# Mirror rows scattered four at a time, and three more split units a batch, in a Fourier-mixing and maxout kernel

## The chip, the cores and the metric

The kernel runs on one core of one Trainium2 chip. The metric is the device time of one execution in microseconds; lower is better. Before the change the median of three runs is 394.58 us (394.48 to 395.24).

## What is computed

```python
def _attn_ref(x):                      # x: 8 x 3072 x 256, float32
    X = np.fft.fft(x, axis=1)
    X = np.fft.fft(X, axis=2)
    return X.real.astype(np.float32)

def _moe_ref(x, w1, w2, w3, w_out):    # x: 24576 x 256; w1..w3: 256 x 768; w_out: 768 x 256
    h = np.maximum(np.maximum(x @ w1, x @ w2), x @ w3)
    return (h @ w_out).astype(np.float32)
```

The output of the first is the input of the second, its eight batches of 3072 rows laid one behind another. The result is 24576 rows of 256 float32.

## The kernel before

**Mirror.** The input is real, so row k and row 3072 - k of a batch's transform are made of the same even part and the same odd part, once added and once subtracted. The kernel computes the parts for k from 0 to 1536 and gets two rows of the output from each, a plus row and a minus (mirror) row. `tE` and `tO` hold the parts for 1536 values of k as columns, `te_tab` and `to_tab` the cosines and sines for them. The one k that is left over is done by `Mix.end` and `l2_mid`.

**Order of the columns.** The 1536 columns are ordered by residue: 96 columns with k = r mod 32 for r = 1, then for r = 2, and so on (`ramp`, `kvec`), with the residues 0, 16 and half of 15 at the end. A matmul of `Mix.k` (L466) has one residue's columns as moving data, and `_parts` lists them for each 512 columns. `_runs` says which rows of the output a slot of 128 columns holds.

**Units.** A batch has three blocks of 512 columns and six chunks of 128 hidden units; one block and chunk make a unit, so a batch has 18 units, numbered u = 0 to 17 here, and the kernel 144 (`g`). A unit that is not split multiplies both parts with two combined weight matrices into two PSUM banks (`unit_plus`, L490 and L491), takes the maximum through `stmp` on ScalarE (L503) and VectorE (L504) into `hp`, then adds one more product to each bank (`unit_minus`, L497), which turns the plus columns into minus columns, and takes the maximum into `hm`: six matmuls of 512 columns. A split unit does the third weight matrix apart: `third` (L819, L821) computes its even and odd products once, VectorE makes `even` (L824), ScalarE `odd` (L823), and GpSimd adds and subtracts them (L828, `plus` and `minus`). What is left is one bank, with its maximum in one VectorE instruction (L837 for `hp`, L849 for `hm`): five matmuls. `third` of a unit is issued two units ahead. Odd units from 7 on are split. A split unit's bank comes from `ps_l1`; the others take one from `ps_l1` and one from `ps_w3` or `ps_o`.

**Second layer and output.** `l2_block` is a generator: it multiplies a finished block's `hp` and `hm` with `w_out` while the next block's six units run, ten steps a unit. For each slot of 128 columns it makes one PSUM tile `po` with 256 plus and 256 minus columns, and VectorE adds the linear part into `ot` (L541). Plus rows go out by plain stores from SP, two or three a slot (L549). Minus rows go out by an indirect DMA from GpSimd (`scatter`, L622), one a slot of 128 rows of 1 KB, 127 rows for a block 2's last slot, with the row numbers in `rows_m`; a one-element memset (L626) follows each. `waiting` holds the slots whose scatter is due; `scatter()` empties it in each unit, after `third`.

**Order of the work.** The order on each engine is written out by hand (`manual_schedule`): a loop over the 144 units which issues the units' products, `third`, the scatters, ten steps of the second layer and whatever `plan` holds for this unit: the loads of x, the mirroring of x (`turn`), and the next batch's first transform (pieces `s`), the store and load that transpose it (`y`, `z`), its table products (`k`) and broadcasts (`v`). The tail, `l2_last`, does the last block of the last batch and spreads its stores over the queues of ScalarE, SP and GpSimd.

Of the kernel before, what the change touches and what calls it, by code (L numbers as in the profile page):

```python
# [29 lines left out]
def _runs(slot):  # L30

    if slot == 11:
        return [(0, 48, 0), (48, 96, 16), (96, 128, 15 + 32 * 64)]
    t, u = divmod(slot, 3)
    edge, r = 96 - 32 * u, 4 * t + 1 + u
    return [(0, edge, r + 32 * 32 * u), (edge, 128, r + 1)]


def _parts(g):

    cols = [(r, 96 * (r - 1), 96 if r < 15 else 64, 0) for r in range(1, 16)]
    cols += [(0, 1408, 48, 0), (16, 1456, 48, 0), (15, 1504, 32, 64)]
    done = []
    for (r, c, wd, _) in cols:
        a, z = max(c, 512 * g), min(c + wd, 512 * g + 512)
        if a < z:
            done.append(((r - 1) % 16 if r < 16 else 16, a - 512 * g, z - a))
    return done
# [3 lines left out]
def kernel(  # L52
# [9 lines left out]
    nc = tc.nc  # L62
# [52 lines left out]
    rows_m = consts.tile([128, 12 * B], INT32, tag="rows_m")  # L115
# [50 lines left out]
    kvec = gen.tile([128, NHALF + 1], FP32, tag="kvec")  # L166
    kv = kvec[:, 0:1440].rearrange("p (r j) -> p r j", j=96)

    def ramp(r):
        n = {0: 6, 6: 5, 11: 4}[r]  # L170
        iota(kv[:, r:r + n, :], [[1, n], [32, 96]], base=r + 1)

    dvec = gen.tile([128, 128], FP32, tag="dvec")
    for c, (s0, s1) in enumerate(FIRST):
        for h in range(2):
            load_x(0, s0, s1, h)
        if c == 0:
            iota(dvec, [[1, 128]])
        elif c < 3:
            ramp((0, 6)[c - 1])  # L180
# [12 lines left out]
    ramp(11)  # L193
    iota(kvec[:, 1408:1504].rearrange("p (r j) -> p r j", r=2), [[16, 2], [32, 48]])
    iota(kvec[:, 1504:NHALF], [[32, 32]], base=15 + 32 * 64)
    iota(kvec[:, NHALF:NHALF + 1], [[0, 1]], base=NHALF)
# [72 lines left out]
    q = gen.tile([128, NHALF + 1], FP32, tag="q")  # L269
# [118 lines left out]
    class Mix:  # L388
# [72 lines left out]
        def k(self, which, g, evict=nc.scalar.copy):  # L461

            tab = (te_tab, to_tab)[which]
            ps2 = ps_f.tile([128, 512], FP32, name="ps2", tag="ps")
            for (i, c0, wd) in _parts(g):
                nc.tensor.matmul(ps2[:, c0:c0 + wd], self.col(i, which),  # L466
                                 tab[:, g * 512 + c0:g * 512 + c0 + wd], start=True, stop=True)
            evict(out=(self.tE, self.tO)[which][:, g * 512:(g + 1) * 512], in_=ps2)  # L468
            if which and (self.b or g):
                cs = slice(g * 512, (g + 1) * 512)  # L470
                nc.sync.dma_start(out=vds[self.b % 2][:, cs], in_=self.tO[0:1, cs])
# [38 lines left out]

    def l2_hidden(po, hcols):
        for jc in range(NJC):
            nc.tensor.matmul(po, hcols(jc), wout_bf[:, jc * 256:(jc + 1) * 256],  # L513
                             start=False, stop=(jc == NJC - 1), skip_group_check=True)
            yield

    def l2_block(b, blk, hp, hm, te, to):

        base = b * S
        for sub in range(4):  # L520
# [3 lines left out]
            if sub % 2 == 0:  # L524
# [10 lines left out]
            ot = out_pool.tile([128, 512], FP32, name="ot", tag="ot")  # L535
# [6 lines left out]
                out=ot.rearrange("p (h c) -> p h c", h=2),  # L542
                in0=po.rearrange("p (h c) -> p h c", h=2),
                in1=lin.unsqueeze(1).to_broadcast([128, 2, 256]), op=ALU.add)
            lo = 1 if slot == 11 else 0
            waiting.append((b * 12 + slot, lo, ot))
            for (p0, p1, k0) in _runs(slot):
                row = base + k0
                stored(nc.sync.dma_start(out=out[row: row + 32 * (p1 - p0 - 1) + 1: 32, :],  # L549
                                         in_=ot[p0:p1, 0:256]), "direct", ("scattered",))  # L550

    def l2_last(hp, hm, te, to, flipped):

        base = (B - 1) * S
        ter, tor = flipped
        for sub in (3, 0, 1, 2):
            slot = 8 + sub
            cp = slice(slot * 128, slot * 128 + 128)
            sp = slice(sub * 128, sub * 128 + 128)
            sm = slice((3 - sub) * 128, (4 - sub) * 128)  # L560
            ot = out_pool.tile([128, 512], FP32, name="ot", tag="ot")
            for (h, tev, tov, wo, hid) in (
                    (0, te[:, cp], to[:, cp], gw[:, 256:512], lambda jc: hp[:, jc, sp]),
                    (1, ter[:, sm], tor[:, sm], gw[:, 512:768], lambda jc: hm[:, jc, sm])):
                if h == 0 or sub == 2:
                    po = ps_o.tile([128, 512], FP32, name="po", tag="po")
                ph = po[:, h * 256:(h + 1) * 256]
                nc.tensor.matmul(ph, tev, gw[:, 0:256], start=True, stop=False)
                yield
                nc.tensor.matmul(ph, tov, wo, start=False, stop=True)  # L570
                yield
                yield from l2_hidden(ph, hid)
                if sub == 2:
                    nc.vector.tensor_copy(out=ot[:, h * 256:(h + 1) * 256], in_=ph)
            if sub != 2:
                nc.vector.tensor_copy(out=ot, in_=po)
            stores = [(p0, p1, base + k0, 0) for (p0, p1, k0) in _runs(slot)]
            for (p0, p1, k0) in _runs(slot):
                if k0 == 0:
                    p0, k0 = 1, 32  # L580
                stores.append((128 - p1, 128 - p0, base + S - k0 - 32 * (p1 - p0 - 1), 256))
            for k, (p0, p1, row, c) in enumerate(stores):
                eng = (nc.scalar, nc.sync, nc.gpsimd)[(k + (sub == 2)) % 3]
                stored(eng.dma_start(out=out[row: row + 32 * (p1 - p0 - 1) + 1: 32, :],
                                     in_=ot[p0:p1, c:c + 256]), "direct", ("scattered",))

    def l2_mid():
# [20 lines left out]
        for _ in l2_hidden(po[0:B, 0:256], lambda jc: hmid[:, jc, :]):  # L608
            pass
        ot = out_pool.tile([128, 512], FP32, name="ot", tag="ot")  # L610
        nc.vector.tensor_copy(out=ot[0:B, 0:256], in_=po[0:B, 0:256])
        stored(nc.sync.dma_start(out=out[NHALF: NHALF + S * (B - 1) + 1: S, :],
                                 in_=ot[0:B, 0:256]), "direct", ("scattered",))
# [4 lines left out]
    def scatter():  # L618

        while waiting:  # L620
            at_row, lo, ot = waiting.pop(0)
            stored(nc.gpsimd.indirect_dma_start(  # L622
                out, bass.IndirectOffsetOnAxis(
                    ap=rows_m[0:128 - lo, at_row: at_row + 1], axis=0),
                ot[lo:128, 256:512], None), "scattered", ("scattered", "direct"))
            nc.gpsimd.memset(mark, 0.0)  # L626
# [60 lines left out]
    m.c(1, 7)  # L687
# [9 lines left out]
    def rows():  # L697

        rows_f = gen.tile([128, 12 * B], FP32, tag="rows_f")
        iota(rows_f.rearrange("p (b t u) -> p b t u", t=4, u=3), [[S, B], [-4, 4], [-1025, 3]],  # L700
             base=S - 1, cm=-32)
        rows_v = rows_f.rearrange("p (b r) -> p b r", r=12)
        adj = gen.tile([128, 12], FP32, tag="adj")
        adv = adj.rearrange("p (t u) -> p t u", u=3)
        four = pidx.to_broadcast([128, 4])
        pool = nc.gpsimd
        for u in range(3):
            scal(adv[:, :, u], four, float(96 - 32 * u), ALU.is_ge, 3071.0, ALU.mult, eng=pool)
        low = gen.tile([128, 2], FP32, tag="low")
        scal(low[:, 0:1], pidx, 47.0, ALU.is_ge, 1520.0, ALU.mult, eng=pool)  # L710
        scal(low[:, 1:2], pidx, 95.0, ALU.is_ge, -511.0, ALU.mult, eng=pool)
        scal(low[:, 0:1], low[:, 0:1], 2031.0, ALU.add, eng=pool)
        pool.tensor_tensor(out=adj[:, 11:12], in0=low[:, 0:1], in1=low[:, 1:2], op=ALU.add)
        pool.tensor_tensor(out=rows_v, in0=rows_v,
                           in1=adj.unsqueeze(1).to_broadcast([128, B, 12]), op=ALU.add)
        pool.tensor_copy(rows_m, rows_f)
# [6 lines left out]
    out_pool = ctx.enter_context(tc.tile_pool(name="outbuf", bufs=6))  # L723
# [45 lines left out]
    for (u, fn) in ((0, lambda: table(2, 512, 1024)), (0, lambda: m.c(7, 16)),  # L769
# [6 lines left out]
                    (3, lambda: table(2)), (3, lambda: table(0)), (5, rows),  # L776
                    (4, lambda: m.k(1, 2)), (4, lambda: m.k(0, 2)), (4, m.end),
                    (5, column), (5, lambda: next(second)), (6, lambda: m.v(2))):
# [5 lines left out]
    for b in range(2, B):  # L784
# [3 lines left out]
        for ch in range(8):  # L788
# [7 lines left out]
             6: ("z0",), 7: ("z1",), 11: ("x",), 12: ("kO0",), 13: ("v0", "kE0", "kO1"),  # L796
# [8 lines left out]
    def is_split(g):  # L805
        return g % 2 == 1 and 7 <= g < B * UNITS
# [23 lines left out]
    def begin(g, dst):  # L830

        te, to, _, jc = operands(g)
        if is_split(g):
            pse2 = ps_l1.tile([128, TOKB], FP32, name="pse2", tag="pse2")
# [20 lines left out]
    for g in range(B * UNITS):  # L855
# [13 lines left out]
        if prev is not None and is_split(prev[0]):  # L869
            finish(*prev)  # L870
            prev = None
# [53 lines left out]
```

## Time and profile before

| What | Value |
|---|---|
| Median of three runs | 394.58 us |
| The profiled execution, its own time | 395.75 us |
| Its span in the profile | 393.8 us |
| TensorE busy | 377.7 us (96%) |
| VectorE busy | 315.0 us (80%) |
| ScalarE busy | 263.0 us (67%) |
| GpSimd busy | 332.9 us (85%) |
| DMA | 54.20 MB, mean 138 GB/s |
| Granted TensorE clock | 0.996 |

A profile's line of a group has the line of the kernel, the engine, the operation, what is written and read, the shapes and the count; behind the bar the busy time in us, the mean of one instruction in ns, and the idle time of the engine before them with what ended it. In a timeline a line starts with its start and length in us; a bracket holds the idle time before it. In the chain of waits each piece is the time that it adds to the chain. A row of the table of stretches has its borders, the busy time and count of TensorE, weight loads, VectorE, ScalarE and GpSimd, the clock, the DMA share and GB/s. PE is TensorE, PEld its weight loads, DVE is VectorE, ACT ScalarE, POOL GpSimd, SP the sync engine.

### The profile page before, as it was taken

How to read it: one execution, taken by the hardware profiler on the slowest of the kernel's cores; microseconds unless marked ns; L12 is line 12 of the kernel's file. 1: busy time of each engine (PE TensorE's matmuls, PEld its weight loads, DVE VectorE, ACT ScalarE, POOL GpSimd, SP SyncE). 2: the span in 40 equal slices, each digit the busy share in tenths (PEclk: the TensorE clock that was granted, in tenths of full speed). 3: DMA queues.
4: the chain of work that ended last, by engine and by line, in shares of the span. 5: the costliest groups of instructions: out<-in, count | busy, mean ns of one | idle time of the engine just before them, and what ended most of it. 6: DMA issues, size and time to landing. Idle time of an engine off the chain costs nothing.

```text
span 393.8 us, 8383 instructions
## 1 busy us (share of the span) xinstructions
PE 377.7 (96%) x2710; PEld 235.9 (60%) x2759; DVE 315.0 (80%) x530; ACT 263.0 (67%) x476; POOL 332.9 (85%) x432
## 2 busy tenths in 40 slices
PE   6698999999999999999999999999999999999994
PEld 2354566566665666565665666556665666666673
DVE  7788897788687788788787888877887887887972
ACT  6877788677766887577867787578866447435420
POOL 8985698979978899889988899889977898869993
PEclk9999999999999999999999999999999999999998
DMA  7999576585838776495767876495333553321234
GB/s 115 159 194 183 131 191 146 114 191 150 161 102 144 190 153 144 117 206 137 137 150 120 210 132 160 118 206 124 108 108 101 131 147 90 94 77 47 90 96 131
DMA packets 66901, 54.20 MB, mean 138 GB/s; under 512 B 32702, under 2 KB 62556, under 8 KB 66003
## 3 DMA queue, kind: packets, MB, share of 16 engines
q0 software_dynamic: 24368, 26.53, 35.5%
q1 hardware_dynamic: 41978, 26.72, 27.0%
q8 instruction: 21, 0.34, 0.4%
q10 hardware_dynamic: 512, 0.43, 0.4%
q14 instruction: 22, 0.18, 0.1%
HBM read 36.95 MB, written 30.81 MB: 172 GB/s over the span
## 4 chain that ended last, share of the span: by engine, by line
PE 84%; DMA 4%; DVE 4%; ACT 3%; issue 2%; POOL 2%; SPq 1%; DVEq 0%; ACTq 0%; POOLq 0%
PE po L513 30%; PE pse L497 12%; PE pse L490 8%; PE pse L491 7%; PE po L536 4%; PE d L821 4%; PE pse L835 4%; PE e L819 3%; PE ps L466 3%; PE pse L836 3%; PE pl L528 2%; PE ps L401 2%; DMA yb<-db 2%; DMA xt<-in_x_dram 2%; ACT tb L405 1%
## 5 line engine op out<-in xcount | busy, mean ns | idle before, releaser
L503 ACT ACTIVATE stmp<-pse 128x512 bf16<-128x512 f32 x150 | 89.6, 600 | 66.1 <-PE pse L497 50.9
L622 POOL DMA_INDIRECT out_dram<-ot,rows_m x92 | 102.4, 1113 | 17.9 <-issue 8.8
L828 POOL TENSOR_TENSOR plus<-even,odd 128x512 bf16<-128x512 f32 x69 | 87.8, 1272 | 32.9 <-DVE even L824 32.7
L828 POOL TENSOR_TENSOR minus<-even,odd 128x512 bf16<-128x512 f32 x69 | 87.5, 1268 | 0.0
L513 PE MATMUL po<-wout_bf,hp 128*128 128x256 bf16 x576 | 86.1, 273 | 0.4
L837 DVE SCALAR_TENSOR_TENSOR hp<-pse,plus 128x512 bf16<-128x512 f32 x69 | 47.6, 689 | 46.5 <-PE pse L836 13.9
L513 PE MATMUL po<-wout_bf,hm 128*128 128x256 bf16 x576 | 78.6, 273 | 0.0
L513 PEld LDWEIGHTS <-hp 128*128 128x128 bf16 x576 | 56.4, 98 | 26.1
L497 PE MATMUL pse<-tO,gd_all 128*128 128x512 bf16 x217 | 70.5, 379 | 1.1 <-DVE hp L504 0.2
L513 PEld LDWEIGHTS <-hm 128*128 128x128 bf16 x576 | 56.4, 98 | 16.3
L541 DVE TENSOR_TENSOR ot<-po,even 128x512 f32<-128x512 f32 x92 | 62.7, 681 | 0.0
L504 DVE TENSOR_TENSOR hp<-pse,stmp 128x512 bf16<-128x512 f32 x75 | 51.4, 685 | 10.1 <-ACT stmp L503 8.7
L490 PE MATMUL pse<-tE,g_all 128*128 128x512 bf16 x148 | 56.0, 379 | 1.9 <-DVE tE L468 0.5
L504 DVE TENSOR_TENSOR hm<-pse,stmp 128x512 bf16<-128x512 f32 x75 | 51.5, 687 | 7.4 <-ACT stmp L503 4.1
L824 DVE SCALAR_TENSOR_TENSOR even<-vb,wcol,e 128x512 f32<-128x512 bf16 x69 | 50.8, 737 | 0.0
L491 PE MATMUL pse<-tO,g_all 128*128 128x512 bf16 x131 | 49.6, 379 | 0.2 <-issue 0.2
L849 DVE SCALAR_TENSOR_TENSOR hm<-pse,minus 128x512 bf16<-128x512 f32 x69 | 47.0, 681 | 0.7
L823 ACT ACTIVATE odd<-d 128x512 f32<-128x512 f32 x69 | 41.3, 598 | 6.2
L134 ACT COPY xt<-xt 64x762 bf16<-64x762 bf16 (+1 forms) x48 | 40.2, 838 | 1.1
L497 PEld LDWEIGHTS <-gd_all 128*128 128x128 bf16 x219 | 21.3, 97 | 22.2 <-issue 4.1
L536 PE MATMUL po<-gw,tO 128*128 128x512 bf16 x85 | 32.3, 380 | 0.0
L405 ACT CAST tb<-ps 128x512 bf16<-128x512 f32 x38 | 20.5, 588 | 14.1 <-PE ps L401 14.1
(175 smaller groups left out, 475.7 us busy)
## 6 DMA issues: line engine op xcount, KB each, us to landing
xt<-in_x_dram POOLq DMA_DIRECT2D x14, 384.0 KB, 8.4
out_dram<-ot SPq DMA_DIRECT2D x55, 96.0 KB
out_dram<-ot SPq DMA_DIRECT2D x64, 64.0 KB
db<-tb SPq DMA_DIRECT2D x21, 192.0 KB
vb<-vd SPq DMA_DIRECT2D x23, 128.0 KB
xt<-in_x_dram POOLq DMA_DIRECT2D x7, 400.0 KB, 6.9
xt<-in_x_dram POOLq DMA_DIRECT2D x7, 368.0 KB, 6.1
out_dram<-ot SPq DMA_DIRECT2D x62, 32.0 KB
```

Source lines behind the costliest of these rows:

```text
L490: nc.tensor.matmul(pse[:, 0:n], g_all[:, jc, 2 * i, :], te, start=True, stop=False)
L491: nc.tensor.matmul(pse[:, 0:n], g_all[:, jc, 2 * i + 1, :], to, start=False, stop=True)
L497: nc.tensor.matmul(pse, gd_all[:, jc, i, :], to, start=False, stop=True, skip_group_check=True)
L503: nc.scalar.activation(out=stmp[:, 0:n], in_=pses[0][:, 0:n], func=AX.Relu)
L504: nc.vector.tensor_tensor(out=dst, in0=src3, in1=stmp[:, 0:n], op=ALU.max)
L513: nc.tensor.matmul(po, hcols(jc), wout_bf[:, jc * 256:(jc + 1) * 256], start=False, stop=(jc == NJC - 1), skip_group_check=True)
L536: nc.tensor.matmul(po, to[:, cp], gw[:, 256:768], start=True, stop=True)
L541: nc.vector.tensor_tensor(out=ot.rearrange("p (h c) -> p h c", h=2), in0=po.rearrange("p (h c) -> p h c", h=2), in1=lin.unsqueeze(1).to_br ...
L622: stored(nc.gpsimd.indirect_dma_start(out, bass.IndirectOffsetOnAxis(ap=rows_m[0:128 - lo, at_row: at_row + 1], axis=0), ot[lo:128, 256:51 ...
L824: nc.vector.scalar_tensor_tensor(out=even3, in0=vb, scalar=wcol[:, jc:jc + 1], in1=e3, op0=ALU.mult, op1=ALU.add)
L828: nc.gpsimd.tensor_tensor(out=dst, in0=even3, in1=odd3, op=op)
L837: nc.vector.scalar_tensor_tensor(out=dst, in0=pse2, scalar=0.0, in1=sums[g][0], op0=ALU.max, op1=ALU.max)
```

## The change

- **Columns.** Each block's four slots are ordered anew. In blocks 0 and 1 partition j of the four slots holds four neighbouring rows for j below 96 (k = 32 j + r with r from `FIRST_OF`: 4 to 7 in block 0, 8 to 11 in block 1; in block 2, 1 to 3, with the multiples of 16 as its fourth), and partitions 96 to 127 hold rows 12 to 15 mod 32. The row left over for `Mix.end` is now k = 0. `Mix.k` gets 8, 8 and 9 matmuls for its three parts instead of 6, 6 and 8.
- **Output.** A block's four slots are collected in one buffer of 8 KB a partition, plus rows in the lower half, minus rows in the upper half in falling order, so that four minus rows of a partition are 4 KB that lie together in the output too. Three such buffers are used in turn; two of them lie where the tables were made. Plus rows go out by two stores a block (three in block 2). Minus rows go out by one scatter a block in blocks 0 and 1, 128 indices of 4 KB, and by three in block 2: 96 rows of 3 KB, 32 of 4 KB and 95 of 1 KB. All are issued when the block's fourth slot is done. `rows_m` has 5 columns instead of 96; the batch comes in by an offset.
- **Splits.** Units 0, 4 and 8 of each batch from the second on are split too, twelve a batch instead of nine. An even split unit takes its bank from `ps_w3`. Where two split units follow one another the second begins before the first is finished, otherwise as before.
- **Tail and places.** `l2_last` works its slots in the order 1, 2, 3, 0 and stores the first three together; `z` of later batches is issued in unit 5 instead of 6 and 7; a few copies at the start are merged.

```diff
+FIRST_OF = (4, 8, 1)
 def _parts(g):
...
+    done = [(12 + i - 1, slice(128 * i + 96, 128 * i + 128)) for i in range(4)]
+    for i in range(4 if g < 2 else 3):
+        done.append((FIRST_OF[g] + i - 1, slice(128 * i, 128 * i + 96)))
+    if g == 2:
+        done += [(16, slice(384, 480, 2)), (15, slice(385, 480, 2))]
     return done
...
+    def ramp(g):
+        kv = kvec[:, 512 * g:512 * g + 512].rearrange("p (s c) -> p s c", s=4)
+        n = 4 if g < 2 else 3
+        iota(kv[:, 0:n, 0:96], [[1, n], [32, 96]], base=FIRST_OF[g])
+        iota(kv[:, :, 96:128], [[1, 4], [32, 32]], base=12 + 1024 * g)
...
+    obufs = [t.rearrange("p (f c) -> p f c", c=256)
+             for t in (obuf, kq[:, 0:2048], kq[:, 2048:4096])]
+    fours = out.rearrange("(n q) d -> n (q d)", q=4)
...
+    def stores_plus(b, blk, buf, s0=0, s1=4):
+
+        mine, v = rows_of(b)
+        r, n = FIRST_OF[blk], s1 if blk < 2 else min(s1, 3)
+        yield v[0:96, r + s0:r + n, :], buf[0:96, s0:n, :]
+        yield v[32 * blk:32 * blk + 32, 12 + s0:12 + s1, :], buf[96:128, s0:s1, :]
+        if n < s1:
+            yield mine[16:NHALF + 1:16, :], buf[0:96, 3, :]
+
+    def stores_minus(b, blk, buf):
+
+        flat = buf.rearrange("p f c -> p (f c)")
+        if blk < 2:
+            return [(b * S + 1, blk, 0, 128, flat[:, 1024:2048])]
+        return [(b * S + 1, 2, 0, 96, flat[0:96, 1280:2048]),
+                (b * S + 1, 3, 0, 32, flat[96:128, 1024:2048]),
+                (b * S, 4, 0, 95, flat[0:95, 1024:1280])]
...
             nc.vector.tensor_tensor(
-                out=ot.rearrange("p (h c) -> p h c", h=2),
-                in0=po.rearrange("p (h c) -> p h c", h=2),
+                out=buf[:, sub:8 - sub:7 - 2 * sub, :], in0=po.rearrange("p (h c) -> p h c", h=2),
                 in1=lin.unsqueeze(1).to_broadcast([128, 2, 256]), op=ALU.add)
-            lo = 1 if slot == 11 else 0
-            waiting.append((b * 12 + slot, lo, ot))
-            for (p0, p1, k0) in _runs(slot):
...
+        for (dst, src) in stores_plus(b, blk, buf):
+            store(nc.sync, dst, src)
+        waiting.extend(stores_minus(b, blk, buf))
...
-        for sub in (3, 0, 1, 2):
+        for sub in (1, 2, 3, 0):
...
+                    if sub == 3:
+                        stores = [*stores_plus(B - 1, 2, buf, 1, 4),
+                                  *stores_turned(B - 1, buf, 1, 4)]
+                for k, (dst, src) in enumerate(stores):
+                    store((nc.scalar, nc.sync, nc.gpsimd)[k % 3], dst, src)
...
         while waiting:
-            at_row, lo, ot = waiting.pop(0)
+            row, col, p0, p1, src = waiting.pop(0)
             stored(nc.gpsimd.indirect_dma_start(
-                out, bass.IndirectOffsetOnAxis(
-                    ap=rows_m[0:128 - lo, at_row: at_row + 1], axis=0),
-                ot[lo:128, 256:512], None), "scattered", ("scattered", "direct"))
+                fours, bass.IndirectOffsetOnAxis(ap=rows_m[p0:p1, col:col + 1], axis=0),
+                src, None, element_offset=256 * row), "scattered", ("scattered", "direct"))
             nc.gpsimd.memset(mark, 0.0)
...
-             6: ("z0",), 7: ("z1",), 11: ("x",), 12: ("kO0",), 13: ("v0", "kE0", "kO1"),
+             5: ("z0", "z1"), 11: ("x",), 12: ("kO0",), 13: ("v0", "kE0", "kO1"),
...
     def is_split(g):
-        return g % 2 == 1 and 7 <= g < B * UNITS
+        if g % 2 == 0:
+            return UNITS <= g < B * UNITS and g % UNITS in (0, 4, 8)
+        return 7 <= g < B * UNITS
...
         if is_split(g):
-            pse2 = ps_l1.tile([128, TOKB], FP32, name="pse2", tag="pse2")
+            if g % 2:
+                pse2 = ps_l1.tile([128, TOKB], FP32, name="pse2", tag="pse2")
+            else:
+                pse2 = ps_w3.tile([128, TOKB], FP32, name="pse3", tag="pse3")
...
-        if prev is not None and is_split(prev[0]):
+        if prev is not None and is_split(prev[0]) and not is_split(g):
             finish(*prev)
             prev = None
```

## The prediction

> **What bounds the kernel now.** I read the page first (engine totals, the chain that ended last), then the chain in order of time, then the timelines of GpSimd and VectorE around the place where the change puts most new work.
>
> ```profile
> span 393.8 us, 8383 instructions
> PE 377.7 (96%) x2710; PEld 235.9 (60%) x2759; DVE 315.0 (80%) x530; ACT 263.0 (67%) x476; POOL 332.9 (85%) x432
> PE 84%; DMA 4%; DVE 4%; ACT 3%; issue 2%; POOL 2%; SPq 1%; DVEq 0%; ACTq 0%; POOLq 0%
> L622 POOL DMA_INDIRECT out_dram<-ot,rows_m x92 | 102.4, 1113 | 17.9 <-issue 8.8
> L828 POOL TENSOR_TENSOR plus<-even,odd 128x512 bf16<-128x512 f32 x69 | 87.8, 1272 | 32.9 <-DVE even L824 32.7
> ```
>
> TensorE carries 84% of the chain. From 65 to 380 us the view of waits holds two waits of TensorE, 0.2 us each, so every column that it streams there is time. GpSimd is the next in load, and its largest job is the mirror scatter. Now the chain and the two other engines at one batch's units 6 to 10:
>
> ```profile
> 226.23 0.22 PE pse L835
> 227.96 0.66 PE po L513 x6
> 228.62 0.28 PE pse L497
> 230.42 0.35 PE po L536
> 230.99 0.36 PE pse L835
> ```
> ```profile
> 219.93 1.27 POOL L828 TENSOR_TENSOR plus<-even,odd 128x512 bf16<-128x512 f32 x1 [1.01 <-DVE even L824]
> 221.16 1.26 POOL L828 TENSOR_TENSOR minus<-even,odd 128x512 bf16<-128x512 f32 x1
> 222.58 0.99 POOL L622 DMA_INDIRECT out_dram<-ot,rows_m  x1 [0.16 <-issue]
> 223.56 0.09 POOL L626 MEMSET mark<- 1x1 f32 x1
> 223.87 2.54 POOL L622 DMA_INDIRECT out_dram<-ot,rows_m  x1 [0.22 <-DVE hm L504]
> 226.41 0.09 POOL L626 MEMSET mark<- 1x1 f32 x1
> 226.47 1.28 POOL L828 TENSOR_TENSOR plus<-even,odd 128x512 bf16<-128x512 f32 x1
> ```
> ```profile
> 223.60 0.74 DVE L824 SCALAR_TENSOR_TENSOR even<-vb,wcol,e 128x512 f32<-128x512 bf16 x1
> 227.78 0.69 DVE L837 SCALAR_TENSOR_TENSOR hp<-pse,plus 128x512 bf16<-128x512 f32 x1 [1.65 <-PE pl L528]
> ```
>
> `even` of unit 9 is ready at 224.34, but GpSimd is in the scatter of slot 11 (2.54 us) and starts unit 9's `plus` at 226.47. VectorE stands idle for 1.65 us until it ends (the view blames PE; `plus` ends at 227.74, `hp` starts at 227.78) and finishes `hp` at 228.47. TensorE's next matmul, the `minus` product of unit 9 (L497), takes 0.28 instead of 0.22 us, and two later ones take 0.35 and 0.36 for 0.22: 0.07 + 0.13 + 0.14 = 0.34 us lost. One slow scatter at unit 6 has used up the slack of this place.
>
> **What the change takes off TensorE.** A unit costs six 512-column matmuls, a split one five. Three more splits in each of seven batches: 21 x 0.2155 us (L490 and L491 pieces, 0.21 to 0.22) = 4.5 us, 0.65 a batch, all on the path. ScalarE loses six `stmp` and gains three `odd` a batch; it has slack (67%).
>
> **What it adds to TensorE.** The table products go from 6, 6 and 8 matmuls of the same 512 columns to 8, 8 and 9.
>
> ```profile
> 235.74 0.23 PE ps L466 x6
> 243.61 0.25 PE ps L466 x8
> ```
>
> In the second, three 96-column matmuls are 3 x 0.040 us by streaming, so the five of 32 to 64 columns took 0.13, or 0.026 each, twice what 32 columns need. New: 4 x 0.040 + 4 x 0.026 = 0.27, twice, and 3 x 0.040 + 6 x 0.026 = 0.28: 0.82 for 0.72 a table, 0.2 us a batch with both tables. The stride-2 columns may cost more or nothing; 0 to 0.1 us a batch.
>
> **GpSimd, in total.** Out: 12 scatters a batch, 11 at 0.98 and one at 2.55, each with 0.31 around it (0.22 idle, 0.09 memset): 17 us. In: five scatters and three pairs `plus`/`minus` (1.23 + 1.21 from start to start): 7.3 us. On a total the load falls by about 2.5 us in 45. What matters is where the five stand.
>
> **GpSimd, in place.** Before, a block's scatters come one at a time as its four slots end. Now they come together, in the unit after the block's last slot: one in unit 0 and one in unit 12, but block 2's three (96, 32 and 95 rows) all in unit 6, behind unit 8's `plus`/`minus` and ahead of unit 9's. Units 8 and 9 are both split now. Clock zero at the start of unit 5; a unit's second layer takes 1.09 us of TensorE.
> - TensorE: unit 5 has 5 matmuls and ends at 2.16, unit 6 (7) at 4.75, unit 7 (6) at 7.1, unit 8 (3) at 8.9, unit 9 (5) at 11.0. Unit 10 begins with unit 9's `minus` product, which needs `hp` of unit 9.
> - VectorE, at 0.60 to 0.66 from start to start: unit 8's `even` ends at 5.1, so its `plus` starts at 5.2.
> - GpSimd: 5.2 + 2.65 (219.93 to 222.58) = 7.9 first scatter; +1.29 = 9.2 second; +1.29 = 10.5 third; plus its own time, plus 0.06, then `plus` of unit 9 for 1.27, `hp` 0.04 later for 0.69.
>
> The 96- and 32-row scatters I take at 0.98, the row of 11 in 12. The 95-row one lies between 0.98 and 2.55 (127 rows, which also starts on partition 1 and lands after 12.2 us, the 128-row one before it after 4.8). 95 is odd like the slow one and starts on partition 0 like the fast ones; I take 1.4, nearer the many. Then `plus` starts at 11.9, `hp` ends at 13.9, and TensorE, due at 11.0, stands 2.9 us. VectorE then has six instructions queued that it should have done (`hp`, `hm`, `even`, the output's sum, `hm`, `hp` of unit 10; 3.7 us), which holds unit 10's `minus` product for another 0.45. Per batch 3.4 us, seven times.
>
> The Trainium skill has a rule on this ("DMA: Bandwidth & Descriptors", section "Why a DMA increments its semaphore by 16 and not by 1"): a DMA is spread over the largest number of engines up to 16 that divides its row count, so 127 rows get one, 96 and 32 get 16, 95 gets five. The late landing of the 127-row scatter agrees. An estimate from that page: with 19 rows an engine against 8 and 127, the 95-row scatter would cost 1.1 us on GpSimd and the sum below would be 2 us lower.
>
> The other runs of splits I checked the same way: `plus` is ready ahead of `hp` by 0.6 us (unit 1), 1.1 (unit 5) and more elsewhere, with the single scatter and the loads of x in between. VectorE gains three `even` (2 us a batch, 60 instructions of 0.6 in 44 us); without the burst that fits, and if it didn't, the cost would be of the size of the 0.45.
>
> **The rest.** The merged stores replace SP's 25 issues a batch by 7; the next writer of a buffer comes three blocks (45 us) later; the z loads go to unit 5, ahead of block 2's stores on SP, and their reader is in unit 11: nothing, as long as the y writes of unit 3 have landed by then (some 4 us later; if not, SP holds back the stores behind them, and their buffers have 45 us). Start: two iotas more on GpSimd ahead of x's loads, 0.15 us. End: before, three slots of the last block were stored as each was done; now 768 KB go out together about 1.8 us before the last matmul, 256 KB follow.
>
> ```profile
> 388.00:390.00 2.00, 0.42 (x4) 0.13 (x2) 0.42 (x1) 0.00 (x0) 0.70 (x2) 1.00 0.64 188
> 390.00:392.00 2.00, 0.00 (x0) 0.00 (x0) 0.00 (x0) 0.00 (x0) 0.00 (x0) 0.68 0.40 101
> ```
>
> 101 GB/s for 2 us at some 190 means that data ended near 391.1. Now 1.05 MB start near 388.7: at 260 GB/s, the best slice of that stretch, they end 1.6 us later, at 190 3.1 later; with larger packets perhaps 0.5. I take 1.5.
>
> **Sum.** Per batch 3.4 - 0.65 - 0.34 (slot 11's stall, gone) + 0.2 = +2.6; seven batches +18.2; batch 0's tables +0.2, start +0.15, end +1.5: +20 us. The profiled execution took 395.75 us (span 393.8, 1.95 around it), so about 416 in profile; on the median of 394.58 it is 414.6.
>
> **Rivals.**
> 1. *Cheap scatters, still slower.* If a scatter costs what a plain store costs on GpSimd (0.50 to 0.57 for 32 to 96 rows at L584), `plus` of unit 9 starts 1.9 earlier: stall 1.1 + 0.45, net +0.7 a batch, 400 to 402 in all. For: those rows. Against: no scatter in 92 is under 0.96. Chance 0.2.
> 2. *Cost by bytes.* Rows of 3 and 4 KB instead of 1: 3.9 us for a block's scatter, 2.2 for the 96 rows; unit 9 waits 4.7, unit 15 another 1: about 430. For: nothing here has rows over 1 KB. Against: x loads (L127) in one long run per partition cost GpSimd 0.57, in 24 short ones 0.78. The upper end of the 95-row scatter alone (2.55) gives 423. Above 426: 0.08.
> 3. *Faster.* The burst is hidden and only TensorE's columns count: 7 x (-0.65 - 0.34 + 0.2) + 0.35 + 1.5 = -3.7, 391. It decides at three scatters within about 1.4 us, gaps of 0.9 included (up to 1.65 the savings still pay), that is under 0.3 us each; or at a slack of unit 9 that I have not seen. For: the total load of GpSimd falls. Against: slot 11 alone exhausts the slack now, and units 8 and 9 get shorter by 0.6 us. Chance 0.14.
> 4. *Nothing to be told*, within 0.2% (0.8 us, about what a measurement tells from no change): 0.02.
>
> **Numbers.** Forecast (403 to 426) 0.56, rival 1 0.2, rival 2 0.08, rival 3 0.14, rival 4 0.02. Faster 0.14, same 0.02, slower 0.84. The range of 400 to 426 reaches from rival 1 to the upper 95-row price with a longer end, and leaves rival 3 and rival 2 out.
>
> **What would show it.** Right: in each batch from the second on three DMA_INDIRECT in a row in unit 6, the next `plus` late, a VectorE idle of 3 to 4 us before `hp` (L837's successor), and waits of TensorE's gd_all product for `hp`, seven times about 3 us; 90 `plus`/`minus` pairs for 69; table products of 0.27 and 0.28. Wrong: scatters well under 0.98 us, or no TensorE wait at unit 10; then the time falls to rival 1 or 3. A GpSimd near 100% would mean rival 2.

## The result and the profile after

The changed kernel takes 415.41 us (median of four runs, 414.81 to 416.12), the kernel before 394.79 us beside it: 1.0516 times as long, 95% interval 1.0503 to 1.053. The prediction was 414.6 us, with a range of 400 to 426. The profiled execution took 414.81 us with a span of 412.7, which is 18.9 us over the span before.

The page of the changed kernel (L845 is `plus` and `minus`, L649 the scatter, L857 `hp` of a split unit, L491 the `minus` product):

```profile
span 412.7 us, 8101 instructions
PE 383.0 (93%) x2818; PEld 237.9 (58%) x2818; DVE 328.6 (80%) x551; ACT 249.2 (60%) x454; POOL 312.2 (76%) x361
PE 65%; POOL 18%; DVE 8%; issue 4%; ACT 2%; DMA 2%; DVEq 0%; POOLq 0%; ACTq 0%
L845 POOL TENSOR_TENSOR plus<-even,odd 128x512 bf16<-128x512 f32 x90 | 114.6, 1273 | 78.7 <-DVE even L841 65.7
L649 POOL DMA_INDIRECT out_dram<-kq,rows_m x29 | 28.9, 997 | 7.4 <-issue 4.0
```

The scatters alone, in the view of the tile `rows_m` (shortest, median and longest in ns, first and last start in us):

```profile
L649 POOL DMA_INDIRECT out_dram<-kq,rows_m x29: 860/991/1137, 72.4 to 400.9; - x29
L649 POOL DMA_INDIRECT out_dram<-obuf,rows_m x8: 985/1032/1083, 57.6 to 390.9; - x8
```

GpSimd has 90 `plus` and 90 `minus` for 69, 37 scatters for 92, and is less busy than before: 312 us for 333. Yet it now carries 18% of the chain that ended last, where it had 2%. Its load fell and its order became the bound. The views of waits from 65 us on, of TensorE and of VectorE:

```profile
PE pse L491 <- DVE hp L857: 16.6, 7, 2.4
```
```profile
DVE hp L857 <- POOL plus L845: 23.4, 7, 3.5
```

Each has its seven waits, one in each batch from the second on. One of them, at a batch's units 6 to 10, in the timelines of GpSimd, VectorE and TensorE:

```profile
231.09 1.28 POOL L845 TENSOR_TENSOR minus<-even,odd 128x512 bf16<-128x512 f32 x1
232.52 0.98 POOL L649 DMA_INDIRECT out_dram<-kq,rows_m  x1 [0.15 <-issue]
...
233.81 0.90 POOL L649 DMA_INDIRECT out_dram<-kq,rows_m  x1 [0.22 <-issue]
...
235.02 1.13 POOL L649 DMA_INDIRECT out_dram<-kq,rows_m  x1 [0.22 <-issue]
236.15 0.09 POOL L652 MEMSET mark<- 1x1 f32 x1
236.21 1.26 POOL L845 TENSOR_TENSOR plus<-even,odd 128x512 bf16<-128x512 f32 x1
```
```profile
237.50 0.69 DVE L857 SCALAR_TENSOR_TENSOR hp<-pse,plus 128x512 bf16<-128x512 f32 x1 [3.28 <-POOL plus L845]
```
```profile
238.25 0.38 PE L491 MATMUL pse<-tO,gd_all 128*128 128x512 bf16 x1 [2.36 <-DVE hp L857]
```

`minus` of unit 8, the 96-, 32- and 95-row scatters, `plus` of unit 9, `hp` of unit 9, `minus` product of unit 9: each starts when the one before it is done. This is the prediction's chain, piece by piece. The table products, in the chain in order of time, and the end, in the table of stretches:

```profile
245.47 0.27 PE ps L460 x8
253.49 0.31 PE ps L460 x9
```
```profile
408.00:410.00 2.00, 0.00 (x0) 0.00 (x0) 0.00 (x0) 0.00 (x0) 0.00 (x0) 1.00 0.77 226
410.00:412.00 2.00, 0.00 (x0) 0.00 (x0) 0.00 (x0) 0.00 (x0) 0.00 (x0) 0.88 0.02 7
```

Something that the prediction did not have shows in the stretches around another of the seven waits. The column behind GpSimd is the granted clock:

```profile
186.00:188.00 2.00, 1.56 (x12) 0.98 (x10) 0.00 (x0) 1.41 (x3) 1.78 (x5) 1.00 0.82 277
188.00:190.00 2.00, 0.08 (x1) 0.08 (x1) 0.82 (x2) 0.49 (x1) 2.00 (x2) 0.91 0.40 132
190.00:192.00 2.00, 2.00 (x5) 0.63 (x5) 2.00 (x4) 0.60 (x1) 1.10 (x2) 0.50 0.01 4
```

TensorE stood idle from 187.6 to 189.9. From 189.6 its clock is 0.50 for 3.41 us, and five matmuls take the 2 us that otherwise hold nine (2 / 0.2155). This happened after three of the seven waits (189.6, 285.2 and 380.8 us). The batch around the first took 48.34 us from table product to table product and that around the second 48.41, the batches with full clock 47.1: 1.3 us for each. Two of the four runs show a mean clock of 0.986, as this trace does, and take 414.8 us; the other two show 0.981 and take 416.0 and 416.1: by the arithmetic one such stretch more (half of 3.41 us is 0.4% of the span) and 1.2 us longer.

### The profile page after: what moved, and what is told of

The parts are those of the page before. It is cut to its first block, busy times and chain, and to the rows that moved or that the text cites. A ratio compares the mean times of both kernels' runs of the same rounds, so it can differ in the third digit from the quotient of the medians.

```text
span 412.7 us, 8101 instructions
## 1 busy us (share of the span) xinstructions
PE 383.0 (93%) x2818; PEld 237.9 (58%) x2818; DVE 328.6 (80%) x551; ACT 249.2 (60%) x454; POOL 312.2 (76%) x361
## 4 chain that ended last, share of the span: by engine, by line
PE 65%; POOL 18%; DVE 8%; issue 4%; ACT 2%; DMA 2%; DVEq 0%; POOLq 0%; ACTq 0%
PE po L546 21%; PE pse L491 8%; POOL plus L845 7%; POOL out_dram L649 5%; PE pse L484 5%; PE pse L485 5%; POOL minus L845 4%; PE pse L855 4%; PE po L569 3%; DVE hp L857 3%; PE pse L856 3%; PE ps L460 3%; PE d L838 3%; PE e L836 3%; PE ps L395 3%
## 5 line engine op out<-in xcount | busy, mean ns | idle before, releaser
L845 POOL TENSOR_TENSOR plus<-even,odd 128x512 bf16<-128x512 f32 x90 | 114.6, 1273 | 78.7 <-DVE even L841 65.7
L845 POOL TENSOR_TENSOR minus<-even,odd 128x512 bf16<-128x512 f32 x90 | 114.5, 1272 | 0.0
L857 DVE SCALAR_TENSOR_TENSOR hp<-pse,plus 128x512 bf16<-128x512 f32 x90 | 61.9, 688 | 53.4 <-PE pse L856 28.5
L497 ACT ACTIVATE stmp<-pse 128x512 bf16<-128x512 f32 x108 | 64.4, 600 | 49.7 <-PE pse L485 29.0
L491 PE MATMUL pse<-tO,gd_all 128*128 128x512 bf16 x198 | 66.7, 382 | 16.6 <-DVE hp L857 16.6
L841 DVE SCALAR_TENSOR_TENSOR even<-vb,wcol,e 128x512 f32<-128x512 bf16 x90 | 66.3, 737 | 0.0
L498 DVE TENSOR_TENSOR hp<-pse,stmp 128x512 bf16<-128x512 f32 x54 | 37.0, 684 | 7.8 <-ACT stmp L497 4.4
L484 PE MATMUL pse<-tE,g_all 128*128 128x512 bf16 x108 | 42.2, 391 | 0.8 <-DVE tE L462 0.4
L574 DVE TENSOR_TENSOR kq<-po,even 128x512 f32<-128x512 f32 x60 | 40.9, 682 | 0.0
L649 POOL DMA_INDIRECT out_dram<-kq,rows_m x29 | 28.9, 997 | 7.4 <-issue 4.0
L855 PE MATMUL pse<-tE,g_all 128*128 128x512 bf16 x90 | 34.3, 381 | 0.1
L836 PE MATMUL e<-tE,g_all 128*128 128x512 bf16 x90 | 34.1, 379 | 0.0
```

What stands on the lines that cost most here:

```text
L484: nc.tensor.matmul(pse[:, 0:n], g_all[:, jc, 2 * i, :], te, start=True, stop=False)
L491: nc.tensor.matmul(pse, gd_all[:, jc, i, :], to, start=False, stop=True, skip_group_check=True)
L497: nc.scalar.activation(out=stmp[:, 0:n], in_=pses[0][:, 0:n], func=AX.Relu)
L498: nc.vector.tensor_tensor(out=dst, in0=src3, in1=stmp[:, 0:n], op=ALU.max)
L841: nc.vector.scalar_tensor_tensor(out=even3, in0=vb, scalar=wcol[:, jc:jc + 1], in1=e3, op0=ALU.mult, op1=ALU.add)
L845: nc.gpsimd.tensor_tensor(out=dst, in0=even3, in1=odd3, op=op)
```

## The experiments

Theory A is the prediction's: three scatters stand ahead of unit 9's `plus` in GpSimd's queue. Theory B says that VectorE cannot carry three split units in a row, theory C that the merged stores, the large rows or the table products cost the time.

**One scatter a unit.** The queue's order alone is changed.

```diff
-        while waiting:
+        if waiting:
             row, col, p0, p1, src = waiting.pop(0)
```

> The changed kernel with one scatter a unit instead of all that wait: block 2's three go out in units 6, 7 and 8, each behind that unit's plus/minus. Everything else stays, all twelve splits too. Theory A (three scatters queued ahead of unit 9's plus on GpSimd): unit 9's plus can start about 9.0 us after the start of unit 5, just in time; the wait of TensorE at unit 10 falls from 2.4 us to under 0.2, the clock stays at 1.0, and the time falls by 7 x 2.8 (wait and queue behind it) and by about 3 x 1.3 (stretches of half clock): 391 to 394 us. Theory B (VectorE can't carry three split units in a row): over 408 us. Theory C (the merged stores, large rows or the table products): about 415 us.

Measured: 393.87 us, ratio to the kernel before 0.9975 (0.9963 to 0.9987). All twelve splits, the stores and the tables stayed, and 21.5 us went: theories B and C fall. TensorE's waits for `hp` are gone from the view of waits, and so is the half clock until the end of the run. All that this view holds of TensorE from 65 to 380 us, and VectorE's line:

```profile
PE pse L856 <- issue: 1.0, 6, 0.2
PE e L836 <- DVE even L841: 0.8, 1, 0.8
```
```profile
DVE hp L857 <- POOL plus L845: 10.0, 14, 0.9
```

`plus` is still late for `hp` 14 times, 0.9 us at most and 10.0 in all, where the changed kernel had seven of 3.3; that fits the slack but for a few losses of 0.1 to 0.2 us.

**No even splits.**

```diff
-            return UNITS <= g < B * UNITS and g % UNITS in (0, 4, 8)
+            return UNITS <= g < B * UNITS and g % UNITS in ()
```

> The changed kernel without the even splits: nine split units a batch as before, the new columns, stores and merged scatters stay. Theory A: with no plus/minus of unit 8 in unit 6 the three scatters end about 9.1 us after the start of unit 5, when unit 9's plus is due at about 9.2: no wait; 394.6 us less 2.4 (slot 11's stall gone) plus 1.8 (tables) plus 0.4 (start) = 394 to 395.5. Theory B: the same. Theory C: over 404 us.

Measured: 395.63 us, ratio 1.0022 (1.0014 to 1.0031): 0.1 over the upper end that was expected. Its batches take 44.98 us, the kernel before 44.91, where -0.34 for slot 11's stall and +0.23 for the tables should have given 44.8, 0.18 less. Most of that is a loss that did not go: of the three that made up the 0.34, the chain still has the third, 0.14 us at unit 11's first product (0.36 for 0.22), in five of the seven batches from the second on. The columns, stores and merged scatters without the splits are thus worth nothing here and cost 0.8 us.

**Even splits 0 and 4 only.** The set is (0, 4).

> The changed kernel with the even splits of units 0 and 4 only, eleven a batch. Theory A: as without even splits, less 14 matmuls of 0.2155 = 3.0 us: 391 to 392.5. Theory B: the run 3, 4, 5 is still there and costs as much as 7, 8, 9, so over 405 us. Theory C: over 404 us.

Measured: 393.79 us, ratio 0.9972 (0.996 to 0.9983). Theory B falls again: with the run of units 3, 4, 5 the time is not over 405 us. The time lies 1.3 us above what was expected. A batch is 0.33 us shorter than with nine splits, where two matmuls are 0.43, and in the chain five of the seven batches from the second on have two of the three losses behind unit 9, 0.12 and 0.14 us, not none as was expected.

**Unit 10 instead of unit 8.** The set is (0, 4, 10).

> The changed kernel with unit 10 split in place of unit 8: twelve splits a batch, three in a row at 9, 10 and 11, the three scatters still together in unit 6. Theory A: the scatters stand ahead of unit 9's plus but no longer behind unit 8's, so plus is ready about when hp can start (10.35 against 10.0 on the clock from unit 5), and TensorE doesn't wait: 391 to 393.5 us. Theory B: as slow as with unit 8, over 408 us. Theory C: about 415 us.

Measured: 394.07 us, ratio 0.9982 (0.997 to 0.9993), 0.6 above the expected range. Twelve splits, three in a row and the three scatters together in unit 6, and no large wait: only where `plus` of unit 8 stands ahead of the scatters is the queue too long. What is left are seven short waits of `minus` products for `hp`:

```profile
PE pse L491 <- DVE hp L857: 1.4, 7, 0.2
```

**Scatters in quiet units.** Units 8 and 10 have no `plus`/`minus` to start.

```diff
-        scatter()
+        scatter({0: 3, 8: 1, 10: 3, 12: 3}.get(u, 0))
         l2_some(10)
```

> The changed kernel, all twelve splits, with block 2's scatters moved to units in which GpSimd has no plus/minus to start: the 96-row one in unit 8, the other two in unit 10. Theory A: no instruction of TensorE waits for GpSimd any more, the waits of 0.1 to 0.2 us at units 9 to 12 that one scatter a unit still had go too (about 2 us in all), and the 21 matmuls show: 1.5 to 2.5 us under the run with one scatter a unit, 391.3 to 392.5. If three splits in a row cost VectorE something of their own (theory B in small), it stays at 393.5 to 394.

Measured: 390.64 us, ratio 0.99 (0.9884 to 0.9917), better than expected. VectorE's view of waits has two waits left for `plus`:

```profile
DVE hp L857 <- POOL plus L845: 2.1, 2, 1.2
```

A batch takes 44.29 us, 0.69 less than with nine splits: three matmuls of 0.2155 are 0.65. None of the three losses behind unit 9 is left in the chain. With GpSimd's order mended the splits are worth 5.0 us against the run without even splits, at least what the prediction's first term said, 4.5.

**Matmuls in the idle time.**

```diff
+        if u == 10 and b:
+            filled.append(ps_l1.tile([128, TOKB], FP32, name="pse2", tag="pse2"))
+            for _ in range(10):
+                nc.tensor.matmul(filled[0], g_all[:, jc, 0, :], operands(g)[0],
+                                 start=True, stop=True)
         if prev is not None and is_split(prev[0]) and not is_split(g):
```

The tile is the one that unit 10's first bank takes afterwards.

> The changed kernel with ten matmuls of 512 columns more (2.16 us, their result is overwritten) on TensorE ahead of unit 9's minus product, where it stands idle 2.4 us per batch. If the stretches of 3.4 us at half clock that follow three of the seven idle times come from the idle time, they vanish, the clock reads 1.0 from start to end, and the time falls by 3 or 4 times 1.3 us to 410 to 412, although TensorE has 15 us more work. If they come from the load or from the chip, the clock stays at 0.986 and the time at 415 or more.

Measured: 410.86 us, ratio 1.0407 (1.039 to 1.0424), 4.6 us less than the changed kernel, with 70 matmuls more. Between the profiled executions the span falls by 3.8 us, from 412.7 to 408.9, which is 1.27 for each of the three stretches. TensorE's timeline has the ten where it stood idle:

```profile
234.60 2.32 PE L893 MATMUL pse<-tE,g_all 128*128 128x512 bf16 x10
237.14 0.38 PE L491 MATMUL pse<-tO,gd_all 128*128 128x512 bf16 x1 [0.22 <-DVE hp L858]
```

The clock is 1.0 up to the end of the last matmuls and every batch from the third on takes 47.0 to 47.1 us. The half clock came from the idle time.

**89 rows for 95.**

```diff
-                (b * S, 4, 0, 95, flat[0:95, 1024:1280])]
+                (b * S, 4, 0, 89, flat[0:89, 1024:1280])]
```

> The changed kernel with 89 rows in the last scatter instead of 95 (six rows of each batch's output are left out). If a scatter's time on GpSimd goes by the rows that fall on one DMA engine (95 rows on five engines, 89, a prime number, on one), it takes 0.98 + 81 x 0.0132 = 2.05 us instead of 1.13, all 0.9 of it on the wait at unit 10: +6.4 us and one or two more stretches at half clock, 421 to 424 us. If it goes by rows or bytes, it takes 1.1 us and the time stays at 415.

This kernel leaves out six rows of each batch's output. Measured: 420.55 us in one run, half a microsecond under what was expected. GpSimd's timeline, and TensorE's view of waits:

```profile
239.22 2.05 POOL L649 DMA_INDIRECT out_dram<-kq,rows_m  x1 [0.23 <-issue]
```
```profile
PE pse L491 <- DVE hp L857: 23.0, 7, 3.3
```

Six rows fewer take 0.9 us longer, 2.05 us as worked out from eight and 127 rows an engine; it starts on partition 0 like the 95- and 96-row ones, where the 127-row one of the kernel before started on partition 1, so that it is the count that makes it slow. The seven waits grow from 2.4 to 3.3 us each, 6.4 in all. The time rises by 5.7 over the profiled execution of the changed kernel, which has three half-clock stretches as this one has; no further stretch came.

**Thirteen splits.** As with the scatters in quiet units, set (0, 4, 8, 14), block 0's scatter in unit 14.

> As the run with the scatters in quiet units, with unit 14 split too (thirteen a batch) and block 0's scatter moved from unit 12 to unit 14. Seven matmuls less, 1.5 us, if GpSimd (then about 42 of 43.6 us a batch) and VectorE still keep up: 390 to 391. If one of them is full, a wait at unit 14 or 16 takes it back: 392 to 395.

Measured: 389.68 us, ratio 0.9874 (0.9858 to 0.9891), the fastest version here and 0.3 under what was expected. A batch takes 44.07 us, 0.22 less than with twelve, one matmul; the whole run gained 1.0 us on the one with twelve, where seven matmuls are 1.5.

**The splits alone, on the kernel before.** `is_split`, the bank and the order of `finish` as in the change, the rest as before.

> The kernel before with the twelve splits alone: old columns, one scatter of 1 KB rows for each slot. Theory A (GpSimd's queue decides, and a scatter costs by the piece): GpSimd needs 12 x 2.44 for plus/minus, 11 x 1.29 + 2.86 for scatters and about 3 for the rest, 49.4 us a batch, where TensorE needs 44.3: it becomes the bound, 394.6 + 7 x 4.5 = 420 to 430 us, waits spread over many units. If scatters were hidden, 390 to 392.

Measured: 431.74 us (two runs), ratio 1.0935 (1.0892 to 1.0977). The views of waits of TensorE and VectorE:

```profile
PE pse L497 <- DVE hp L842: 27.6, 16, 3.4
```
```profile
DVE hp L842 <- POOL plus L830: 40.4, 24, 4.0
```

Waits at two places a batch and more, five half-clock stretches. It is slower than the total load of GpSimd said (420 to 430): the batches in the middle take 50.9 us where 49.4 were worked out, and the half-clock stretch that each of them holds is 1.3 of the difference. With a scatter for each slot, in this order, GpSimd has no room for the splits; whether another order would make it is not tested.

**Fourteen splits.** Set (0, 4, 8, 12, 14), scatters in units 0, 4, 8 and 14.

> As the run with thirteen splits, with unit 12 split too, and the scatters in units 0, 4, 8 and 14, which have no plus/minus to start. Seven matmuls less (1.5 us), but GpSimd needs 14 x 2.44 + 6.4 + 3 = 43.6 us a batch and TensorE 43.2: it is full. 388.5 if the queue still keeps up, 390 to 396 if it has become the bound.

Measured: 394.07 us, ratio 0.9975 (0.9965 to 0.9984). `plus` is late again:

```profile
DVE hp L857 <- POOL plus L845: 17.5, 22, 1.2
```

In three stretches of 45 us (the fifth busy time of a row is GpSimd's):

```profile
110.00:155.00 45.00, 44.41 (x332) 27.92 (x330) 39.12 (x63) 29.93 (x53) 43.04 (x45) 1.00 0.68 151
155.00:200.00 45.00, 44.41 (x333) 27.93 (x332) 39.13 (x63) 29.92 (x53) 43.02 (x45) 1.00 0.65 151
200.00:245.00 45.00, 44.40 (x336) 27.90 (x334) 39.11 (x63) 29.93 (x53) 43.00 (x45) 1.00 0.64 151
```

GpSimd is busy 43.0 of 45 us, with thirteen splits it was 41.5, and a batch takes 44.9: the queue is all but full, and the gain of the thirteenth is lost with it.

## Why the prediction was right

The likeliest case happened, at its place and by its chain: three scatters in a row, VectorE idle for 3.3 us before `hp`, TensorE waiting seven times. That 414.6 came within 1 us of 415.4 is luck, since a term that the prediction did not have made up for three that it took too large. The terms, as predicted and as measured, for the span's 18.9 us:

| Term | Predicted, us | Measured, us |
|---|---|---|
| TensorE's wait at unit 10, seven times | 7 x 2.9 = 20.3 | 7 x 2.52 = 17.6 |
| VectorE's queue behind it | 7 x 0.45 = 3.2 | 7 x 0.28 = 2.0 |
| Half clock after three of the waits | 0 | 3 x 1.3 = 3.9 |
| Table products | 8 x 0.2 = 1.6 | 8 x 0.23 = 1.8 |
| 21 matmuls less | -4.5 | -4.5 |
| Slot 11's stall gone | -2.4 | -2.4 (not told apart) |
| Start | 0.15 | 0.4 (in one pair of executions) |
| End | 1.5 | 0.1 |
| Sum | 20 | 18.9 |

The sum meets 18.9 because two things outside the table cancel: a batch with full clock grew by 2.2 us where its terms give 2.04, and one batch of the kernel before was 0.67 us longer than the others.

- *The wait* is counted from the moment at which the product was due; the view of waits, which counts from the end of the matmul before it, has 2.37 of the 2.52. It was sized 0.38 too long. 0.27 of it is the 95-row scatter, put at 1.4 between ends of 0.98 and 2.55, measured 1.13; 0.08 is the 32-row one, 0.90 and not 0.98. Here the Trainium skill's rule ("DMA: Bandwidth & Descriptors", section "Why a DMA increments its semaphore by 16 and not by 1"), that a DMA is spread over the largest number of engines up to 16 that divides its rows, gave the better size: 1.1 by the estimate from that page. The run with 89 rows agrees as well, 2.05 us for fewer rows. The count of rows on one engine, not the row count, was the scale to read between 0.98 and 2.55 by.
- *The queue behind it*: two short losses, 0.13 and 0.15 us, at the same two matmuls as before, not one of 0.45.
- *The clock* was missing. It hid the misses above: without it the sum of the other measured terms is 15.0.
- *The end* was mis-sized. The merged stores move 320 GB/s from 402 to 404 us, more than the 260 that I took as the best rate, and their last data land before 410.4 us. The span ends 5.5 us after the last matmul, before it was 5.4. The best stretch:

```profile
402.00:404.00 2.00, 2.00 (x21) 1.79 (x19) 0.94 (x2) 0.00 (x0) 0.00 (x0) 1.00 0.91 320
```

- *The start* can't be told from chance: the first table product begins at 19.3 us before and at 19.7 after, and between 18.8 and 20.0 in the nine other runs that begin with the changed kernel's code.
- *GpSimd's total* was added up wrongly. The five new scatters are some 6.5 us a batch beside the 7.3 of the pairs, so that the load falls by about 3 and not 2.5. Nothing in the sum hangs on it.
- *Rival 1*, scatters at 0.5 us, is out: 0.86 to 1.14 in all 37. *Rival 2*, cost by bytes, is out too: 128 rows of 4 KB take 0.97 to 1.08, as with 1 KB. *Rival 3*, a hidden burst, named the right point of decision: with the order mended the same splits are faster than before, by 1.0%.
- The room for the scatters, "within about 1.4 us" in the prediction, is 1.1 by its own clock (`plus` must start at 11.0 - 0.69 - 0.04 - 1.27 = 9.0, the scatters start at 7.9). One of them about fits, three don't, and that agrees with the run with one scatter a unit: there `plus` of unit 9 is late for `hp`, and TensorE hardly waits.

## What to carry to other kernels

When small transfers are merged, ask in which single place the merged ones will now stand in their engine's queue, and what that queue owes to others right behind it; a lower total load says nothing on that. A wait is cheap to move if the work has no reader of its own: here the choice of the unit in which a scatter is issued made 415 us into 391. And with GpSimd busy 43 of 45 us there was no gain left, although its scatters stood in units without `plus` and `minus` to start.

## What the runs showed of the hardware

- Idle times of TensorE of 2.4 us are enough for a half clock, but only in some places. The stretches begin on a fixed grid of 3.413 us (in the changed kernel their starts lie 28 steps apart, in the run with 89 rows 14 and 29, in the one with the splits alone 14 and 15). In the changed kernel the three steps in which TensorE was idle for 2.1 to 2.4 us were followed by a step at 0.50; the waits that a border of the grid split, with at most 1.7 us in a step, were not. The two other runs agree: steps with 2.1 to 3.3 us idle were all followed by a half clock, steps with 1.9 us and less never. A step need not be wholly idle. The Trainium skill ("TensorE: Matmul & The Clock Gate", section "Part 1: The HAM clock gate (the "warmup" mystery)") has a free-running window of 3413 ns; the grid agrees. Ten matmuls without use in the wait gave back 4.6 us.
- A scatter's time on GpSimd does not change from 1 KB to 4 KB rows (0.96 to 1.14 and 0.97 to 1.08 us for 128 rows), but with the number of rows, and not in its order: about 0.9 for 32, 0.94 to 1.00 for 96, 1.13 for 95, 2.05 for 89, 2.55 for 127.
